# FNet plus top-1 MoE on one core: the products of one spectral unit split in two halves, the second moved behind the next unit

## The chip, the cores and the metric

The kernel runs on one core of one Trainium2 chip. The time is the device time of one execution in microseconds (us); the median of the runs is compared. PE is TensorE (matmuls), DVE is VectorE, ACT is ScalarE, POOL is GpSimd, SP is SyncE, which here issues nearly all loads. "Granted clock" is the share of its full clock that PE was given.

## What is computed

```
xn  = layernorm(x)                                   # x: 2048 x 512
a, b = xn @ dft_hid_re.T, xn @ dft_hid_im.T          # DFT over the hidden axis
y   = dft_seq_re @ a - dft_seq_im @ b                # real part of the DFT over the sequence
h_e = silu(xn @ w1[e]) @ w2[e]                       # 8 experts, 512 -> 1376 -> 512
out = x + y + gate * h_top1                          # each token by its top-1 expert of xn @ w_gate
```

All is float32. The kernel takes the sequence DFT first, on `xn`, and the hidden DFT last.

## The kernel before

**Precision by splitting.** A float32 operand is split into a high half `hi` (a cast, on ACT) and a low half `lo = v - hi` (a subtraction, on DVE), both of the type that PE takes in one pass. A product is then three matmuls: `hi x xh`, `lo x xh`, `hi x xl`, where `xh`, `xl` are the halves of the tokens (lines 537 to 539). One matmul of 128 x 128 by 128 x 512 is the unit of work here.

**Four units.** The sequence DFT's matrix is cut into chunks of 512 output rows; two neighbouring chunks `c` and `c + 1`, of the real matrix (`ri` 0) or of the imaginary one (`ri` 1), make a unit: `UNITS = [(0, 0), (0, 1), (1, 0), (1, 1)]`, pair and `ri`. In a unit a 2 x 2 block scheme saves one product in eight. It has an "even" half, run now, and an "odd" half, run behind the MoE. The even half (`EVEN`, line 522) makes four products for each of eight blocks `b` of 256 input rows: `p1` and `p2` of the block itself ("plain": one load of 512 KB, one cast, one low half), and `q6` and `p3` of sums of blocks ("sums": the plain block and a second load of 512 KB, `other`; three additions, lines 495 to 497; a cast and a low half, lines 470 and 474). Each product of a block is 6 matmuls, so a block has 24, 12 of them on the plain part and 12 on the sums. The two accumulators of each product stand in two PSUM banks; the eight banks hold one unit's four products. When a unit is done, `out_of` copies them on ACT to `raw` tiles and stores them.

**Order of the work.** `add` (line 100) lists all blocks once, in the order in which they are to be loaded and prepared; `need(key, ahead)` (line 104) writes out the preparation of every block up to `ahead` behind the one wanted. A scheduler then orders the instructions of each engine ahead of time, earlier-written ones first among those that it believes ready; each engine works through its own list in order, and an instruction that waits holds all behind it. SP's list is kept in the written order throughout (line 217); DVE's and ACT's are kept so only in the stretches marked `manual_schedule`. Slots: six `raw` tiles (shared by loads and by the stores of results), two `other`, two `sums`, four pairs of `hi` and `lo`.

**The (0,1) unit of before** has a lead: for the first six blocks (`LEAD = 6`) it does the plain products alone, from blocks of their own kind ("c"), two ahead. Meanwhile `between` (line 571) does, block by block, the logits of the router (`logits`, 128 small matmuls), their join and copy (`join_logits`), the choice of expert (`choose`), and the count of tokens per expert (`count`, two small matmuls whose result opens `route`). Then come the sums of these six blocks ("even" with `sums_alone`, line 501), and blocks 6 and 7 with all four products. During that and during the (1,0) unit `go_on` and `during` (lines 905 and 913) do the rest of the routing (`route`, small instructions on DVE in pieces), write the tokens as halves of words (`words`, ACT) and scatter them by expert (`scatter`, POOL, an indirect DMA each). In the (1,1) unit the first expert's window of tokens is loaded on SP, which needs all scatters done. The experts' MoE, the odd halves and the hidden DFT follow.

Of the kernel before, what the change touches and what calls it, by code (L numbers as in the profile page):

```python
# [23 lines left out]
NB = NT // 2  # L24
KD = D // P
TC = 512
# [6 lines left out]
DH = D // 2  # L33
UNITS = [(0, 0), (0, 1), (1, 0), (1, 1)]
PLAIN = 5
LEAD = 6
KS = D // 32


# [9 lines left out]
def fnet_moe(ctx, tc, x, cr, ci, dr, di, wg, w1, w1r, w2, w2r, out):  # L49
    nc = tc.nc  # L50
    V, A, T, G, SY = nc.vector, nc.scalar, nc.tensor, nc.gpsimd, nc.sync
# [9 lines left out]
    def bank(name):  # L61
        return psum.tile([P, 512], F32, tag="bank", name=name)
# [37 lines left out]
    def add(key, fn):  # L100
        order[key] = len(blocks)
        blocks.append((key, fn))

    def need(key, ahead):
        for i in range(len(ready), min(order[key] + 1 + ahead, len(blocks))):
            ready[blocks[i][0]] = blocks[i][1]()
        return ready[key]

    def c_block(c, ri, b):
        src = (cr, ci)[ri][c, b].rearrange("p j t -> p (j t)")  # L110
        add(("c", c, ri, b), lambda: stream(src, P, 1024))
# [14 lines left out]
    for b in range(PLAIN):  # L126
        for c in range(2):
            c_block(c, 0, b)
    for u in range(len(UNITS)):
        if u == 1:  # L130
            for b in range(LEAD):
                c_block(0, 1, b)
            for b in range(LEAD):
                add(("even", 1, b), lambda b=b: (None, sums_alone(b)))
        for b in range((PLAIN, LEAD, 0, 0)[u], NB):
            add(("even", u, b), lambda u=u, b=b: even_sums(u, b))
    for i in range(E):
        for b in range(6):
            for k in range(2):
# [326 lines left out]
    def two_parts(t, cols):  # L466
        hi = st.tile([P, 1024], F32R, tag="hi", name="hi")
        lo = st.tile([P, 1024], F32R, tag="lo", name="lo")
        n = cols.stop - cols.start
        A.copy(hi[:, :n], t[:, cols])  # L470
        return hi, lo, t, cols, n

    def low_parts(hi, lo, t, cols, n):
        V.tensor_sub(lo[:, :n], t[:, cols], hi[:, :n].bitcast(F32))  # L474
        return hi, lo
# [13 lines left out]
    def sums_of(u, b):  # L489
        if not tp:  # L490
            tp.append(ctx.enter_context(tc.tile_pool(name="two", bufs=2)))
        raw, other, t = raw_blocks(u, b, 0)

        def add_up():
            V.tensor_add(t[:, :TC], other[:, :TC], other[:, TC:])
            V.tensor_add(t[:, :TC], t[:, :TC], raw[:, :TC])
            V.tensor_add(t[:, TC:], t[:, :TC], raw[:, TC:])

        return raw, t, add_up

    def sums_alone(b):
        raw, t, add_up = sums_of(1, b)
        add_up()
        return low_parts(*two_parts(t, slice(0, 2 * TC)))

    def even_sums(u, b):
        raw, t, add_up = sums_of(u, b)
        plain = two_parts(raw, slice(0, 2 * TC))
        add_up()
        plain = low_parts(*plain)  # L510
        return plain, low_parts(*two_parts(t, slice(0, 2 * TC)))

    def odd_sums(u, b):
# [8 lines left out]
    EVEN = [(0, 0, 0, "p1"), (0, 1, 2, "p2"), (1, 0, 1, "q6"), (1, 1, 3, "p3")]  # L522
    ODD = [(0, 0, 2, "q4"), (1, 0, 3, "q5"), (1, 1, 1, "p7")]

    def product(todo, key, acc, b0=0, going=(), ahead=3):
        b = key[-1]
        got = need(key, ahead)
        if key[0] == "c":
            got = (got,)
        for m, n, q, name in todo:  # L530
            if name not in acc:
                acc[name] = [bank(f"s{k}") for k in range(2)]
            ch, cl = (v[:, n * TC:(n + 1) * TC] for v in got[m])
            for k in range(2):
                c = (q % 2) * DH + k * P
                a, al = xh[b][:, q // 2, c:c + P], xl[b][:, q // 2, c:c + P]
                T.matmul(acc[name][k], a, ch, start=(b == b0 and name not in going), stop=False)  # L537
                T.matmul(acc[name][k], a, cl, start=False, stop=False)  # L538
                T.matmul(acc[name][k], al, ch, start=False, stop=(b == NB - 1))  # L539

    def out_of(acc, u, names=None):
        for n in names or acc:
            store_pair(ps[n][u], acc[n])

    def unit(kind, u, mid=None, lead=0, between=None, acc=None):
        todo = {"even": EVEN, "odd": ODD}[kind]
        acc = acc or {}
        going = tuple(acc)
        b0 = 0 if u else PLAIN
        for b in range(lead):  # L550
            product(todo[:2], ("c", 0, 1, b), acc, ahead=2)
            between(b)
        for b in range(b0, NB):
            product(todo[2 if b < lead else 0:], (kind, u, b), acc, b0, going)
            if mid:
                mid(b)
        return acc

    plain = two_products(2, pre0)
# [4 lines left out]
    acc = unit("even", 0, go_on_first, acc={"p2": plain[:2], "p3": plain[2:]})  # L564
# [4 lines left out]
    written = ExitStack()  # L569

    def between(b):
        if b < 2:
            if b == 1:
                logits()
                written.enter_context(tc.manual_schedule(engines={A.engine}))
                copy_logits()
            turn_some((), (3 + b,))
            return
        if b == LEAD - 1:
            count()  # L580
        if b > 2:
            spread(b - 3)
            return
        written.close()
        join_logits()
        early.close()
        late.append(early.enter_context(tc.tile_pool(name="late", bufs=1, side="right")))
        zero = late[0].tile([P, D], F32, name="zero")
        G.memset(zero, 0.0)
        for t, base, n in ((xs, S, 3 * P), (hr, WCUM[E], 1)):  # L590
            for r in range(0, n, P):
                m = min(P, n - r)
                tc.keep_in_program_order(A.dma_start(t[base + r:base + r + m, :], zero[:m, :].bitcast(U16)))
        with tc.high_priority(), tc.manual_schedule(engines={V.engine}):
            choose()

    def sm(name, shape, dt=F32):
        return late[0].tile([P] + shape, dt, name=name)
# [4 lines left out]
    def choose():  # L603
        top = sm("top", [NT])
        V.reduce_max(top, lg, axis=AX.X)

        is_top = sm("is_top", [NT, E])
        V.tensor_tensor(is_top, lg, top[:, :, None].to_broadcast([P, NT, E]), op=OP.is_equal)
        V.tensor_mul(is_top, is_top, per_tile(down1))
        ftop = sm("ftop", [NT])  # L610
        V.reduce_max(ftop, is_top, axis=AX.X)
        V.tensor_tensor(oh, is_top, ftop[:, :, None].to_broadcast([P, NT, E]), op=OP.is_equal)

        gd = sm("gd", [NT])
        ge_gr.extend((sm("ge", [NT]), sm("gr", [NT])))
        ge = ge_gr[0]
        V.tensor_sub(gd, top, top)
        A.activation(ge, gd, AF.Exp)
# [10 lines left out]
    routing = []  # L629

    def count():
        cnt = parts4[2]
        ohf = oh.rearrange("p t e -> p (t e)")
        T.matmul(cnt[:, 0:P], ones, ohf, start=True, stop=True)
        T.matmul(cnt[:, P:2 * P], before, ohf, start=True, stop=True)
        routing.append(route(cnt))
        with tc.high_priority():
            next(routing[0])

    def scan(name, t0, n, steps):  # L640

        t = [t0, sm(name, list(t0.shape[1:]))]
        q = 0
        for sh in steps:
            V.tensor_copy(t[1 - q][:, :sh], t[q][:, :sh])
            V.tensor_add(t[1 - q][:, sh:], t[q][:, sh:], t[q][:, :n - sh])
            q = 1 - q
        return t[q]
# [7 lines left out]
    def route(cnt):  # L656
        tot = sm("tot", [NT, E])
        V.tensor_copy(tot.rearrange("p t e -> p (t e)"), cnt[:, 0:P])
        rank = sm("rank", [NT, E])
        V.tensor_sub(rank.rearrange("p t e -> p (t e)"), cnt[:, P:2 * P], tot.rearrange("p t e -> p (t e)"))  # L660
        inc = scan("inc1", tot, NT, (1, 2, 4, 8))
        V.tensor_add(rank, rank, inc)
        num, num1 = sm("num", [E]), sm("num1", [E])
# [234 lines left out]
    def spread(*tiles):  # L898
        for t in tiles:
            words(t)  # L900
            if routing:
                for o in range(len(scat), t + 1):
                    scatter(o)

    def go_on(b):
        spread(*((3,), (4,), (5,), (6,), (7,), (), (), ())[b])
        if b >= LEAD - 1:
            next(routing[0], None)

    acc = unit("even", 1, go_on, LEAD, between)  # L910
    out_of(acc, 1)

    def during(b):
        next(routing[0], None)
        spread(*((8, 9), (10, 11), (12, 13), (14,), (15,), (), (), ())[b])
        if b == 6:
            place(0)

    acc = unit("even", 2, during)
    out_of(acc, 2)  # L920
    early.close()
    norms_on.close()
    mo = ExitStack()
# [15 lines left out]
    acc = unit("even", 3, during_last)  # L939
# [5 lines left out]
    todo = []  # L945
# [123 lines left out]
    for u, mid in enumerate((None, load_ds, first_fetches, last_fetches)):  # L1069
        acc = unit("odd", u, mid)  # L1070
# [143 lines left out]
```

## Time and profile before

| | |
|---|---|
| median of 3 runs | 696.73 us (695.53 to 698.81) |
| the profiled execution | 697.55 us, of which the span from the first to the last instruction is 695.8 |
| PE busy | 684.8 us, 98% of the span |
| DVE busy | 551.1 us, 79% |
| ACT busy | 403.6 us, 58% |
| moved by DMA | 174.31 MB, 251 GB/s in the mean |
| mean granted clock of PE | 0.995 |

A row of the timeline gives the start (us from the span's start), the time taken, the engine, the source line, the operation, the tile written and the tiles read, shapes, a count where equal neighbours are merged, and in brackets how long the engine had been idle before it and what ended that. In a row of waits stand who waited for whom, the total in us, how often, and the longest. In a row of stretches stand the busy time of each engine with its number of instructions, then the granted clock, the busy share of the 16 DMA engines and GB/s. A busy PE says only that matmuls were in flight; their pitch, from one start to the next, tells at what speed.

### The profile page before, as it was taken

The numbers are of one execution on the slowest core, as the hardware profiler recorded it, in microseconds if no ns is written. First come the engines' busy times: TensorE is split into PE (matmuls) and PEld (weight loads), VectorE is DVE, ScalarE is ACT, GpSimd is POOL, SyncE is SP. The second block draws the span as 40 slices with busy tenths as digits, with TensorE's granted clock in tenths as the row PEclk, the third lists the DMA queues.
The fourth block names the chain that finished last, engine by engine and source line by source line (L and its number), as shares of the span: only waits on it lengthen the run. The fifth ranks groups of instructions, "written<-read, shape, count | busy, mean of one in ns | idle before, by whom it ended". The sixth has DMA issues, their size and how long they took to land.

```text
span 695.8 us, 10899 instructions
## 1 busy us (share of the span) xinstructions
PE 684.8 (98%) x3859; PEld 598.7 (86%) x3859; DVE 551.1 (79%) x912; ACT 403.6 (58%) x628; POOL 55.9 (8%) x66
## 2 busy tenths in 40 slices
PE   9999979999999999999999999999999999999997
PEld 7888758888888999999999999999888878888886
DVE  6979869999685767777778697878779799658784
ACT  5684636757557466656666676664556464425342
POOL 1000001418100000000000000000000000222120
PEclk9999989999999999999999999999999999999999
DMA  9464686898893976685985868747496988689775
GB/s 320 179 231 151 218 304 222 340 380 289 257 311 114 303 243 181 220 180 199 264 274 166 282 171 286 251 138 263 144 329 218 350 320 309 233 325 362 250 266 177
DMA packets 88184, 174.31 MB, mean 251 GB/s; under 512 B 40318, under 2 KB 41598, under 8 KB 88125
## 3 DMA queue, kind: packets, MB, share of 16 engines
q1 hardware_dynamic: 77691, 143.02, 63.4%
q10 hardware_dynamic: 7874, 22.16, 8.4%
q0 software_dynamic: 2560, 8.39, 3.4%
q8 instruction: 32, 0.52, 0.3%
q14 instruction: 27, 0.22, 0.1%
HBM read 135.59 MB, written 29.42 MB: 237 GB/s over the span
## 4 chain that ended last, share of the span: by engine, by line
PE 67%; DVE 14%; DMA 12%; ACT 3%; issue 2%; SPq 0%; DVEq 0%; ACTq 0%
PE s L538 7%; PE s L539 7%; PE s L537 7%; PE up L831 6%; PE up L830 6%; PE acc L343 6%; PE up L829 6%; PE y L860 4%; PE y L861 4%; PE y L859 4%; DVE lo L474 2%; PE y L852 2%; PE y L853 2%; PE y L854 2%; DMA raw<-pd 2%
## 5 line engine op out<-in xcount | busy, mean ns | idle before, releaser
L81 DVE TENSOR_TENSOR lo<-raw,hi 128x1024 fp32r<-128x1024 f32 (+2 forms) x109 | 123.0, 1133 | 36.2 <-ACT hi L80 34.4
L538 PE MATMUL s<-lo,xh 128*128 128x512 f32 x366 | 144.1, 394 | 5.0 <-DVE lo L81 4.5
L80 ACT CAST hi<-raw 128x1024 fp32r<-128x1024 f32 (+2 forms) x109 | 106.9, 987 | 62.8 <-PE up L830 34.8
L539 PE MATMUL s<-hi,xl 128*128 128x512 f32 x366 | 143.3, 392 | 0.0
L537 PE MATMUL s<-hi,xh 128*128 128x512 f32 x366 | 140.1, 393 | 0.0
L830 PE MATMUL up<-wtl,hi 128*128 128x256 f32 (+10 forms) x352 | 102.4, 291 | 0.0
L831 PE MATMUL up<-wth,lo 128*128 128x256 f32 (+10 forms) x352 | 102.4, 291 | 0.0
L829 PE MATMUL up<-wth,hi 128*128 128x256 f32 (+10 forms) x352 | 102.3, 291 | 0.0
L470 ACT CAST hi<-sums 128x1024 fp32r<-128x1024 f32 x54 | 57.0, 1055 | 76.2 <-PE s L539 32.9
L538 PEld LDWEIGHTS s<-lo,xh 128*128 128x128 f32 x366 | 69.4, 190 | 21.1 <-DVE lo L81 4.9
L537 PEld LDWEIGHTS s<-hi,xh 128*128 128x128 f32 x366 | 69.2, 189 | 16.5 <-issue 1.7
L474 DVE TENSOR_TENSOR lo<-sums,hi 128x1024 fp32r<-128x1024 f32 x54 | 66.1, 1223 | 21.0 <-ACT hi L470 20.8
L539 PEld LDWEIGHTS s<-hi,xl 128*128 128x128 f32 x366 | 69.4, 190 | 14.4
L829 PEld LDWEIGHTS up<-wth,hi 128*128 128x128 f32 (+1 forms) x352 | 66.0, 187 | 1.3
L830 PEld LDWEIGHTS up<-wtl,hi 128*128 128x128 f32 (+1 forms) x352 | 66.0, 187 | 1.3
L831 PEld LDWEIGHTS up<-wth,lo 128*128 128x128 f32 (+1 forms) x352 | 66.0, 188 | 0.0
L860 PE MATMUL y<-hl,hi 128*128 128x318 f32 (+9 forms) x220 | 65.2, 297 | 0.2 <-DVE hl L837 0.2
L861 PE MATMUL y<-hh,lo 128*128 128x318 f32 (+9 forms) x220 | 65.0, 296 | 0.0
L859 PE MATMUL y<-hh,hi 128*128 128x318 f32 (+9 forms) x220 | 64.2, 296 | 0.0
L1084 POOL DMA_INDIRECT hw<-hr,posr x16 | 20.9, 1306 | 478.2 <-PE s L539 424.0
L833 ACT ACTIVATE sil<-up 128x256 f32<-128x256 f32 (+9 forms) x88 | 35.5, 404 | 32.1 <-PE up L831 17.9
L470 ACT CAST hi<-raw 128x512 fp32r<-128x512 f32 (+1 forms) x48 | 38.9, 811 | 22.6 <-PE s L539 9.4
(232 smaller groups left out, 1288.7 us busy)
## 6 DMA issues: line engine op xcount, KB each, us to landing
raw<-in_w SPq DMA_DIRECT2D x80, 512.0 KB
raw<-in_ci SPq DMA_DIRECT2D x38, 512.0 KB
raw<-in_cr SPq DMA_DIRECT2D x30, 512.0 KB
p<-raw ACTq DMA_DIRECT2D x16, 512.0 KB
other<-in_ci SPq DMA_DIRECT2D x16, 512.0 KB
q<-raw ACTq DMA_DIRECT2D x12, 512.0 KB
other<-in_cr SPq DMA_DIRECT2D x11, 512.0 KB
other<-p SPq DMA_DIRECT2D x10, 512.0 KB
```

The costliest lines, as they stand in the source:

```text
L80: A.copy(hi, raw)
L81: V.tensor_sub(lo, raw, hi.bitcast(F32))
L470: A.copy(hi[:, :n], t[:, cols])
L537: T.matmul(acc[name][k], a, ch, start=(b == b0 and name not in going), stop=False)
L538: T.matmul(acc[name][k], a, cl, start=False, stop=False)
L539: T.matmul(acc[name][k], al, ch, start=False, stop=(b == NB - 1))
L829: T.matmul(t[:m, :w], hi[:, c:c + m], self.xh[:, k, :w], start=(k == 0), stop=False)
L830: T.matmul(t[:m, :w], hi[:, c:c + m], self.xl[:, k, :w], start=False, stop=False)
L831: T.matmul(t[:m, :w], lo[:, c:c + m], self.xh[:, k, :w], start=False, stop=(k == KD - 1))
L859: T.matmul(y, hi[:m, c:c + P], hh[:m, :w], start=first, stop=False)
L860: T.matmul(y, hi[:m, c:c + P], hl[:m, :w], start=False, stop=False)
L861: T.matmul(y, lo[:m, c:c + P], hh[:m, :w], start=False, stop=last)
```

## The change

- The (0,1) unit is cut in two. `plain_half` does the plain products of all eight blocks, from blocks of the "c" kind, two ahead, and stores `p1` and `p2`. Then the whole (1,0) unit runs. Then `unit("alone", 1)` does the sums' products of (0,1), all eight blocks, and stores `q6` and `p3`. The list of blocks is put in that order.
- `between` is called for all eight blocks of the plain half. The count stands behind block 5 as before, now behind the words of that block, and the piece of `route` that ends in the tokens' places (`posi`) is cut off from it by a `yield` and done behind block 6. From `choose` to the end of the plain half DVE's list is kept in the written order (before: only within `choose`, with raised priority).
- The further pieces of `route` are done in the (1,0) unit; words and scatters: tokens' tiles 0 to 4 in the plain half, 5 to 12 in (1,0), 13 to 15 in the sums alone, where also the first expert's place is read.
- In `even_sums` the low half of the plain block is written ahead of the three additions, not behind them.

```diff
-LEAD = 6
+COUNT = 5
...
-    for u in range(len(UNITS)):
-        if u == 1:
-            for b in range(LEAD):
+    for u in (0, 2, 3):
+        for b in range(0 if u else PLAIN, NB):
+            add(("even", u, b), lambda u=u, b=b: even_sums(u, b))
+        for b in range(NB):
+            if u == 0:
                 c_block(0, 1, b)
-            for b in range(LEAD):
-                add(("even", 1, b), lambda b=b: (None, sums_alone(b)))
-        for b in range((PLAIN, LEAD, 0, 0)[u], NB):
-            add(("even", u, b), lambda u=u, b=b: even_sums(u, b))
+            if u == 2:
+                add(("alone", 1, b), lambda b=b: (None, sums_alone(b)))
...
     def even_sums(u, b):
         raw, t, add_up = sums_of(u, b)
-        plain = two_parts(raw, slice(0, 2 * TC))
+        plain = low_parts(*two_parts(raw, slice(0, 2 * TC)))
         add_up()
-        plain = low_parts(*plain)
...
+    def plain_half(mid):
+        acc = {}
+        for b in range(NB):
+            product(EVEN[:2], ("c", 0, 1, b), acc, ahead=2)
+            mid(b)
         return acc
...
-        if b == LEAD - 1:
-            count()
         if b > 2:
+            if b == COUNT + 1:
+                next(routing[0])
             spread(b - 3)
+            if b == COUNT:
+                count()
             return
...
-        with tc.high_priority(), tc.manual_schedule(engines={V.engine}):
-            choose()
+        written.enter_context(tc.manual_schedule(engines={V.engine}))
+        choose()
...
+        yield
         inc = scan("inc1", tot, NT, (1, 2, 4, 8))
...
-    acc = unit("even", 1, go_on, LEAD, between)
+    acc = plain_half(between)
+    written.close()
     out_of(acc, 1)
 
     def during(b):
         next(routing[0], None)
-        spread(*((8, 9), (10, 11), (12, 13), (14,), (15,), (), (), ())[b])
+        spread(b + 5)
+
+    acc = unit("even", 2, during)
+    out_of(acc, 2)
+
+    def meanwhile(b):
+        spread(*((13,), (), (14,), (), (15,), (), (), ())[b])
         if b == 6:
             place(0)
 
-    acc = unit("even", 2, during)
-    out_of(acc, 2)
+    acc = unit("alone", 1, meanwhile)
+    out_of(acc, 1)
```

More of the change, by code (lines that the diff above doesn't have):

```diff
@@ L543, in out_of, with unit @@
             store_pair(ps[n][u], acc[n])
-    def unit(kind, u, mid=None, lead=0, between=None, acc=None):
-        todo = {"even": EVEN, "odd": ODD}[kind]
+    def unit(kind, u, mid=None, acc=None):
+        todo = {"even": EVEN, "odd": ODD, "alone": EVEN[2:]}[kind]
         acc = acc or {}
@@ L549, in unit @@
         b0 = 0 if u else PLAIN
-        for b in range(lead):
-            product(todo[:2], ("c", 0, 1, b), acc, ahead=2)
-            between(b)
         for b in range(b0, NB):
-            product(todo[2 if b < lead else 0:], (kind, u, b), acc, b0, going)
+            product(todo, (kind, u, b), acc, b0, going)
             if mid:
                 mid(b)
+        return acc
+    def plain_half(mid):
[3 more added lines that the diff above has]
+            mid(b)
         return acc
@@ L903, in spread @@
                     scatter(o)
[L905 to L908, printed above, removed]
-    acc = unit("even", 1, go_on, LEAD, between)
+    acc = plain_half(between)
+    written.close()
     out_of(acc, 1)
```

## The prediction

> **What bounds the kernel now.** I read the page's first part first, then the table of what TensorE (PE) waited for, then a table by stretches of 5 us, then the timelines of PE, VectorE (DVE) and ScalarE (ACT) around the one place that stood out.
>
> ```profile
> span 695.8 us, 10899 instructions
> PE 684.8 (98%) x3859; PEld 598.7 (86%) x3859; DVE 551.1 (79%) x912; ACT 403.6 (58%) x628; POOL 55.9 (8%) x66
> ```
>
> PE is busy in all but 11.0 us of the span. Nothing in this change takes away or adds a matmul, so all that it can win is PE's idle time and time in which matmuls ran slowly. The waits of PE, whole run:
>
> ```profile
> PE s L538 <- DVE lo L81: 4.5, 1, 4.5
> PE spare L208 <- DVE eps L211: 1.1, 1, 1.1
> PE s L538 <- DVE lo L474: 0.5, 1, 0.5
> ```
>
> The columns are who waited for whom, total us, times, longest. One wait of 4.5 us is most of what can be had (1.1 is the start). L81 is the low half of a streamed block, so the waiting product is a plain one of the (0,1) unit. The stretches around it (PE busy, weight loads, DVE, ACT, POOL, granted clock, DMA share, GB/s):
>
> ```profile
> 90.00:95.00 5.00, 4.77 (x24) 2.69 (x22) 2.08 (x3) 3.01 (x4) 0.00 (x0) 1.00 0.96 339
> 95.00:100.00 5.00, 0.72 (x2) 0.63 (x3) 4.32 (x7) 1.05 (x2) 0.00 (x0) 0.83 0.92 324
> 100.00:105.00 5.00, 5.00 (x14) 3.83 (x13) 5.00 (x9) 1.14 (x3) 0.53 (x1) 0.50 0.56 218
> 105.00:110.00 5.00, 5.00 (x24) 3.99 (x23) 4.21 (x17) 4.82 (x8) 0.00 (x0) 0.99 0.93 329
> ```
>
> After the gap PE counts as fully busy from 100 to 105, but does 14 matmuls where an undisturbed stretch does 22 (5 us at 0.2267 us each), at a granted clock of 0.50. PE's own rows (start, us):
>
> ```profile
> 94.38 0.39 PE L537 MATMUL s<-hi,xh 128*128 128x512 f32 x1
> 99.28 0.79 PE L538 MATMUL s<-lo,xh 128*128 128x512 f32 x1 [4.52 <-DVE lo L81]
> 99.88 0.63 PE L539 MATMUL s<-hi,xl 128*128 128x512 f32 x1
> ...
> 104.57 0.63 PE L538 MATMUL s<-lo,xh 128*128 128x512 f32 x1
> 105.28 0.39 PE L537 MATMUL s<-hi,xh 128*128 128x512 f32 x1
> ...
> 107.09 0.39 PE L539 MATMUL s<-hi,xl 128*128 128x512 f32 x1
> ```
>
> From 105.28 to 107.09 lie 8 steps of 0.226 us (0.2267 over longer runs: the pitch). 94.38 to 107.09 are the 24 matmuls of plain blocks 4 and 5; at the pitch they take 24 x 0.2267 = 5.44 us, and they took 107.09 + 0.23 - 94.38 = 12.94. **Loss: 7.5 us**: about 4.7 of waiting, and 2.8 of half-speed matmuls.
>
> Why the low half came late (DVE and ACT):
>
> ```profile
> 86.64 0.43 DVE L450 TENSOR_TENSOR tb<-tb,xn 128x256 f32<-128x256 f32 x1
> 91.72 0.69 DVE L495 TENSOR_TENSOR sums<-other 128x512 f32<-128x512 f32 x1 [4.65 <-DMA other<-in_ci]
> ...
> 95.62 0.69 DVE L495 TENSOR_TENSOR sums<-other 128x512 f32<-128x512 f32 x1 [1.75 <-DMA other<-in_ci]
> ...
> 98.01 1.22 DVE L81 TENSOR_TENSOR lo<-raw,hi 128x1024 fp32r<-128x1024 f32 x1
> ```
> ```profile
> 89.94 2.02 ACT L80 CAST hi<-raw 128x1024 fp32r<-128x1024 f32 x2
> ```
>
> Both high halves were made by 91.96. The low half stood in DVE's queue behind the add-ups of two sums blocks, which waited 4.65 and 1.75 us for transfers that the plain blocks do not need.
>
> **The change part by part.** *Plain products first.* Ahead of plain block 4 now stand only plain blocks, each one transfer and one low half; no add-up is issued until plain block 6 asks two ahead. The wait of 4.5 us and the slow clock behind it go: 7.5 us off, if the next-latest thing holds. That is the count: the block after it needs `oh`, made by the chain that starts when the logits are joined.
>
> ```profile
> 90.52 1.06 PE L414 MATMUL part<-turned,sel 128*32 128x512 f32 x8
> ```
> ```profile
> 99.15 0.71 DVE L417 STREAM_TRANSPOSE turned<-part 128x512 f32<-128x512 f32 x1
> ...
> 105.88 0.29 DVE L612 TENSOR_TENSOR oh<-is_top,ftop 128x128 bf16<-128x128 f32 x1
> ```
>
> The join ends at 91.6. The transpose (0.71) and six instructions of at most 0.29 give `oh` near 94.1; the count stands on PE behind plain block 5, which now ends at 94.38 + 5.44 = 99.8. Spare: 5.7 us. The low half of plain block 5, now in order behind `choose`, comes at 94.1 + 0.2 + 1.2 = 95.5, due at 97.1: 1.6 spare. So the plain half runs through, and its blocks 6 and 7 end at 99.8 + 0.1 + 5.44 = 105.4. The logits and the join are unmoved on PE.
>
> *The (1,0) unit* follows: 192 matmuls, 43.5 us, to 148.9. *Then the moved part*: 8 blocks of sums alone, each 12 matmuls, 2.72 us, 21.8 us in all. Each needs two transfers of 512 KB, as this one (1.05 MB together), three additions, a cast and a low half. Before, six such blocks stood in the (0,1) unit, after PE had waited for them.
>
> ```profile
> raw<-in_ci SPq DMA_DIRECT2D x38, 512.0 KB
> ```
>
> DVE's steps at full pace:
>
> ```profile
> 161.46 0.68 DVE L495 TENSOR_TENSOR sums<-other 128x512 f32<-128x512 f32 x1
> 162.06 0.68 DVE L497 TENSOR_TENSOR sums<-sums,raw 128x512 f32<-128x512 f32 x1
> 162.67 1.21 DVE L474 TENSOR_TENSOR lo<-raw,hi 128x1024 fp32r<-128x1024 f32 x1
> 163.80 0.68 DVE L496 TENSOR_TENSOR sums<-sums,raw 128x512 f32<-128x512 f32 x1
> ```
>
> An addition holds DVE 0.60 us, a low half 1.13. A sums block alone is 3 x 0.60 + 1.13 = 2.93 us against 2.72 of PE; a full block is 4.06 against 5.44. Routing, over the stretch that holds it (rows of L474 and of one of the three equal additions):
>
> ```profile
> 107.64:158.59 50.95, 21.84 (x19) 1.00 0.87 320
> ...
> 107.64:158.59 50.95, 7.58 (x11) 1.00 0.87 320
> ```
>
> 50.95 - 19 x 1.13 - 33 x 0.60 = 9.7 us, from the count's first reader to the last table. DVE's account behind the count (100.2): eight full blocks 32.5, eight sums alone 23.4, routing 9.7, two waits for a cast of 1.01 (2.02 for two, above) because DVE now follows the written order through the first two (1,0) blocks, and the last block's own cast 1.0: 68.6, so 168.8. PE wants the last low half at 148.9 + 7 x 2.72 = 167.9. DVE is 0.9 us short if no transfer ever holds it, nothing if PE does the four high products (0.9) first, as it does where a low half is expected late:
>
> ```profile
> 121.25 1.08 PE L537 MATMUL s<-hi,xh 128*128 128x512 f32 x4
> ```
>
> *Transfers there.* SP, the load queue, works in written order, and its raw tiles share six slots with the stores. At the unit boundary of before (1,0 to 1,1):
>
> ```profile
> 174.53 1.06 ACT L363 COPY raw<-s 128x512 f32<-128x512 f32 x2
> ```
> ```profile
> 178.33 0.33 SPq L481 DMA_DIRECT2D raw<-in_ci  x1
> 178.76 0.37 SPq L486 DMA_DIRECT2D other<-in_ci  x1
> ```
> ```profile
> 184.11 0.69 DVE L495 TENSOR_TENSOR sums<-other 128x512 f32<-128x512 f32 x1
> ```
> ```profile
> SPq L481 <- DMA p<-raw: 14.9, 3, 11.1
> ```
>
> The first eviction starts when the first product of the last block is done, 18 matmuls (4.1 us) ahead of the unit's end T = 178.6. The fourth block's raw load was held up to 11.1 us for a store and left at T - 0.3; its first addition ran at T + 5.5. Before, that block was due 16 us after T; a fourth sums block is due at T + 8.2. From its first addition it needs 3 x 0.60 + 1.0 + 1.2 + some 0.2 of hand-overs = 4.2 us: T + 9.7, 1.5 late. The four blocks behind it go at DVE's 2.93 against 2.72: 0.8 more. This and DVE's account are the same queue, so they do not add. I take 2.5 us, near this row's 2.3; the ends are 0 (three blocks ready ahead cover it) and 5.4 (below). The gaps would be under 2 us each; the 0.5 us wait of the list above left the clock alone:
>
> ```profile
> 560.00:565.00 5.00, 4.55 (x21) 3.49 (x20) 5.00 (x7) 2.62 (x4) 0.00 (x0) 1.00 0.94 355
> ```
>
> Gaps between 0.5 and 4.5 us the trace does not show. By the Trainium skill (TensorE: Matmul & The Clock Gate, Part 1) the clock halves only after about 3.4 us idle and recovers after about 3.4 us of work; the trace agrees with the first in its 4.5 us wait and shows a longer recovery, 5.9 us. By that rule gaps under 2 us cost only themselves, as I count them.
>
> *The rest.* The low half written ahead of the add-up in full blocks costs nothing of its own: ACT's cast (1.01) is hidden by PE's three-block lead, and if it is not, 1.0 us for each such block. The eight words and scatters per unit shift later by a few blocks: the last scatter would be issued in the fifth sums-alone block, 10 us ahead of the (1,1) unit, whose second block holds the window load that waits for it; an SP wait there would hold the later loads of (1,1). POOL, whose scatters go in order, then has the same work over a longer stretch. PSUM: the sums alone take four banks, and those that they take over were evicted three products before. I cost these at nothing.
>
> **Sum.** 7.5 - 2.5 = 5.0 us gained. The profiled execution took 697.55 us, 1.75 around its span; the median of the runs is 696.73. 697.55 - 5.0 = 692.55, and on the median **691.7 us**.
>
> **The rivals.** *Transfers bound the sums alone.* From T - 0.3 must arrive five blocks of 1.05 MB, three stores of 0.52 and three scatters of 0.26: 7.6 MB. Over the fullest 25 us of before the 16 engines moved:
>
> ```profile
> 140.00:165.00 25.00, 25.00 (x112) 20.70 (x111) 25.00 (x73) 17.13 (x25) 9.43 (x5) 1.00 1.00 374
> ```
>
> 7.6 MB at 374 GB/s is 20.3 us; the last block lands at T + 20.0, is ready at T + 24.4, due at T + 19.0: 5.4 us lost, 2.1 gained, 694.6. For it: DMA share 1.00 there. Against: three blocks are loaded before T. The Trainium skill (DMA: Bandwidth & Descriptors, Where 436 GB/s comes from) has loads from HBM bound by about 358 GB/s per core; by that figure 0.9 us more would be lost. The 374 here stands above it.
>
> *The plain half still waits.* If the low half of block 4 is ordered behind something slow (the join, the parts of x), a wait of 2 us stays: 2.7 or so of the idle goes, 2.8 of clock may stay or not. With the 2.5 lost later, 0.2 to 3.0 gained: about 695.
>
> *Slower.* The raw load of the fourth sums block is late, as at the boundary from (0,1) to (1,0), 43.5 us ahead of the other, at 135.1:
>
> ```profile
> 137.39 0.33 SPq L481 DMA_DIRECT2D raw<-in_cr  x1
> ```
> ```profile
> 146.77 0.68 DVE L495 TENSOR_TENSOR sums<-other 128x512 f32<-128x512 f32 x1
> ```
>
> There the fourth block's load left at T + 2.3 and its first addition ran at T + 11.7. With the 4.2 us behind it, a sums block would be ready at T + 15.9, 7.7 late; the clock would halve (2.8), and DVE's 0.8 follows: 11.3, of which the gain covers 7.5: 3.8 slower, 700.5. It decides from one gap of about 4.5 us in the sums alone. Against it: DVE was busy with routing in that stretch, and there is little routing left then.
>
> **How the numbers follow.** Forecast 0.60 (0 to 4 us lost: 689.2 to 693.2), transfers 0.18, plain half 0.12, slower 0.10. Under 0.5% (3.5 us) a measurement of this kernel cannot tell from no change. So faster 0.60; same 0.18 + 0.12 = 0.30; slower 0.10. The range goes from 688.8 (nothing lost, and the 0.4 of small waits gone) to 698.5, which leaves out the slower case and little else; the likeliest case alone is 689.2 to 693.2.
>
> **What would show it.** Right: no PE wait on L81, granted clock 1.00 from 85 to 110, the plain half ended near 105; DVE full from the count on; PE waits on L474 in the sums alone, 2 to 3 us in several gaps, clock 1.00. Wrong: a PE wait of over 4 us anywhere in the two units, an SP wait on a store just ahead of the fourth sums block that reaches PE, or DVE waiting for `other` there.

## The result and the profile after

The changed kernel takes 704.25 us in the median (703.96 to 705.15, 4 runs) beside 696.33 for the kernel before (695.53 to 698.81, 4 runs): ratio 1.011, interval 1.0082 to 1.0138. It is slower by 1.1%; 691.7 was forecast. The first part of the page, then the largest of what TensorE (PE) waited for:

```profile
span 702.8 us, 10909 instructions
PE 684.5 (97%) x3859; PEld 598.1 (85%) x3859; DVE 553.1 (79%) x912; ACT 402.1 (57%) x628; POOL 50.3 (7%) x66
```
```profile
PE s L537 <- DVE lo L474: 8.5, 4, 5.5
PE s L536 <- ACT hi L470: 2.5, 2, 2.0
```

The work of PE is the same as before; its idle time went from 11.0 to 18.3 us. The wait on L81 is gone. In its place stand six waits for the halves of blocks (L470 casts a high half, L474 subtracts a low one). Where they lie is read from the same stretches of both kernels (columns as above: PE, weight loads, DVE, ACT, POOL, granted clock, DMA share, GB/s), before first:

```profile
85.00:108.00 23.00, 18.48 (x148) 12.71 (x125) 15.59 (x28) 10.48 (x18) 0.53 (x1) 0.85 0.86 307
108.00:130.00 22.00, 21.93 (x96) 17.61 (x95) 21.73 (x55) 13.58 (x20) 9.45 (x7) 1.00 0.79 281
150.00:185.00 35.00, 35.00 (x156) 29.00 (x155) 31.20 (x47) 26.48 (x38) 20.77 (x9) 1.00 0.82 291
```
```profile
85.00:108.00 23.00, 23.00 (x184) 17.13 (x176) 14.12 (x26) 15.50 (x25) 0.53 (x1) 1.00 0.72 256
108.00:130.00 22.00, 18.17 (x78) 14.07 (x77) 21.83 (x64) 11.10 (x16) 12.93 (x6) 1.00 0.82 299
130.00:150.00 20.00, 20.00 (x90) 16.56 (x89) 20.00 (x61) 11.00 (x16) 5.48 (x4) 1.00 0.73 267
150.00:185.00 35.00, 27.75 (x112) 21.57 (x111) 24.69 (x33) 18.62 (x30) 7.07 (x6) 0.90 0.91 338
```

- *Plain half* (85 to 108): PE never stops and the clock stays at 1.00. Before, 4.5 us of idle and 2.8 of half clock (18.48 x 0.15) lay here: about 7.3 us gained, as forecast (7.5).
- *Start of (1,0)* (108 to 130): 3.83 us idle against 0.07: 3.8 lost. Nothing was forecast here.
- *Sums alone* (from T = 154.3): 7.25 us idle, and a lower clock around the longest gap, by these rows of the changed kernel:

```profile
165.00:170.00 5.00, 1.96 (x8) 0.95 (x6) 0.17 (x1) 1.05 (x1) 0.00 (x0) 0.92 1.03 418
170.00:175.00 5.00, 1.92 (x5) 1.54 (x6) 4.20 (x6) 1.29 (x2) 0.00 (x0) 0.50 1.01 387
175.00:180.00 5.00, 5.00 (x21) 4.12 (x20) 4.97 (x7) 1.85 (x3) 1.20 (x1) 0.89 0.99 351
```

1.96 x 0.08 + 1.92 x 0.50 + 5.00 x 0.11 = 1.7 us of PE's busy time lost to it. 8.9 lost in all; 2.5 was forecast.

7.3 - 3.8 - 8.9 = -5.4 by idle time and clock, while the span grew by 7.0. Idle time hides short waits, because a matmul counts as busy for the 0.39 us that it is in flight, while the next can start 0.2267 us behind it. The starts of matmuls show these waits too: the (1,0) unit takes 48.3 us where 43.5 were forecast, and the sums alone take 31.6 (first and last row below, with the fifth and the sixth block between) where 96 matmuls at the pitch take 21.8.

```profile
154.32 0.39 PE L536 MATMUL s<-hi,xh 128*128 128x512 f32 x1
...
166.35 1.20 PE L536 MATMUL s<-hi,xh 128*128 128x512 f32 x4 [0.60 <-ACT hi L470]
...
176.39 1.09 PE L536 MATMUL s<-hi,xh 128*128 128x512 f32 x4
...
185.94 0.39 PE L536 MATMUL s<-hi,xh 128*128 128x512 f32 x1
```

That is 7.3 - 4.7 - 9.8 = -7.2, and the (1,1) unit starts 7.1 us later than before (185.9 against 178.8).

At the start of (1,0), VectorE's own rows show what stands ahead of the low half that PE wants (the second block's):

```profile
108.68 0.17 DVE L650 COPY inc<-tot 128x8 f32<-128x8 f32 x1
...
112.90 0.17 DVE L677 TENSOR_TENSOR posi<-rrk,rro 128x16 int32<-128x16 f32 x1
113.00 1.23 DVE L474 TENSOR_TENSOR lo<-raw,hi 128x1024 fp32r<-128x1024 f32 x1
```

The chain of the tokens' places holds DVE from 108.68 to 113.0, 4.3 us, and the low half is written behind it. In the sums alone, PE, DVE and then the load queue:

```profile
173.08 0.80 PE L537 MATMUL s<-lo,xh 128*128 128x512 f32 x1 [5.52 <-DVE lo L474]
```
```profile
152.13 0.69 DVE L495 TENSOR_TENSOR sums<-other 128x512 f32<-128x512 f32 x1
...
158.62 0.69 DVE L495 TENSOR_TENSOR sums<-other 128x512 f32<-128x512 f32 x1 [0.89 <-DMA other<-in_ci]
159.35 0.69 DVE L496 TENSOR_TENSOR sums<-sums,raw 128x512 f32<-128x512 f32 x1
...
164.48 0.69 DVE L497 TENSOR_TENSOR sums<-sums,raw 128x512 f32<-128x512 f32 x1
170.47 0.69 DVE L495 TENSOR_TENSOR sums<-other 128x512 f32<-128x512 f32 x1 [5.30 <-DMA other<-in_ci]
171.19 0.69 DVE L496 TENSOR_TENSOR sums<-sums,raw 128x512 f32<-128x512 f32 x1
171.80 1.22 DVE L474 TENSOR_TENSOR lo<-sums,hi 128x1024 fp32r<-128x1024 f32 x1
```
```profile
157.68 0.33 SPq L481 DMA_DIRECT2D raw<-in_ci  x1
166.18 0.33 SPq L486 DMA_DIRECT2D other<-in_ci  x1
```
```profile
SPq L486 <- DVE sums L495: 32.4, 13, 9.5
...
SPq L486 <- DMA p<-raw: 8.1, 1, 8.1
```

This is the old wait in a new place. The additions at 152.13, 158.62 and 170.47 open the third, the fourth and the sixth block. The low half at 171.80 belongs to the fifth block, whose high half ended at 166.3, but it stands in DVE's queue behind additions of the sixth, which wait 5.3 us for `other`. That load left 8.5 us behind the one ahead of it, 8.1 of them spent waiting for a store (last row: the load queue from 95 to 200 us; the row above it shows that most of its waiting is for VectorE to free a tile). Why it waits for a store is told by the list of its waits in the built program, where it is load 66:

```
66 L486 DMA other<-in_ci 128x1024 [waits DMAHW5_49,DMAHW2_49,DVE_49]
```

In that program the loads of SP and the stores of ACT use eight such transfer counters (DMAHW0 to 7) in turn, and counter 2 had last been used by the store of `p2`, issued at 158.0. The tile's own slot had been free since 159.3, when the fourth block's first addition ended.

### The profile page after: what moved, and what is told of

The parts are those of the page before. It is cut to its first block, busy times and chain, and to the rows that moved or that the text cites. A ratio compares the mean times of both kernels' runs of the same rounds, so it can differ in the third digit from the quotient of the medians.

```text
span 702.8 us, 10909 instructions
## 1 busy us (share of the span) xinstructions
PE 684.5 (97%) x3859; PEld 598.1 (85%) x3859; DVE 553.1 (79%) x912; ACT 402.1 (57%) x628; POOL 50.3 (7%) x66
## 4 chain that ended last, share of the span: by engine, by line
PE 80%; DVE 9%; DMA 5%; ACT 4%; issue 1%; ACTq 0%; SPq 0%; DVEq 0%
PE s L537 8%; PE s L538 8%; PE s L536 8%; PE up L837 6%; PE acc L343 6%; PE up L836 6%; PE up L835 6%; PE o L1115 4%; PE o L1113 4%; PE o L1114 4%; PE y L866 4%; PE y L867 4%; PE y L865 4%; DVE lo L474 3%; PE y L858 2%; PE y L859 2%
## 5 line engine op out<-in xcount | busy, mean ns | idle before, releaser
L81 DVE TENSOR_TENSOR lo<-raw,hi 128x1024 fp32r<-128x1024 f32 (+2 forms) x111 | 125.5, 1135 | 40.9 <-ACT hi L80 38.9
L80 ACT CAST hi<-raw 128x1024 fp32r<-128x1024 f32 (+2 forms) x111 | 108.5, 985 | 64.5 <-PE up L836 36.2
L536 PE MATMUL s<-hi,xh 128*128 128x512 f32 x366 | 137.5, 391 | 2.5 <-ACT hi L470 2.5
L470 ACT CAST hi<-sums 128x1024 fp32r<-128x1024 f32 x54 | 56.9, 1053 | 87.8 <-DVE sums L497 37.3
L474 DVE TENSOR_TENSOR lo<-sums,hi 128x1024 fp32r<-128x1024 f32 x54 | 66.0, 1222 | 19.1 <-ACT hi L470 18.8
L1092 POOL DMA_INDIRECT hw<-hr,posr x16 | 18.5, 1158 | 472.8 <-PE s L538 418.6
L470 ACT CAST hi<-raw 128x512 fp32r<-128x512 f32 (+1 forms) x46 | 36.7, 797 | 16.5 <-PE s L538 5.3
```

What stands on the lines that cost most here:

```text
L80: A.copy(hi, raw)
L81: V.tensor_sub(lo, raw, hi.bitcast(F32))
```

## The experiments

A first theory (S) was the ties of loads to stores: by that counter, and by the six `raw` slots that both use. Its rivals were the bytes (B, later T), VectorE's work (D), and the place of the blocks. Each run stands beside runs of the kernel before on its own chip, and the ratio is to these. The kernel before took 695.3 to 696.7 us on these chips, so a difference of two medians from different chips is good to about 1.4 us.

### Is it the ties? x1, x5, x6, y4

**x1**: POOL issues the four stores of (1,0), with counters of other queues. `store_pair(..., by=G)`: `by.dma_start(dst, o)` for `A.dma_start(dst, o)`.

> The changed kernel, with the four stores of the (1,0) unit's results issued by POOL instead of ACT: the same bytes, at the same place, but in the built program SP's loads of the sums-alone blocks then no longer wait for the completion counters that these stores use. Theory A (a load held for a store): the gap of 5.5 us and the 2.8 us of half clock behind it come from the second load of the sixth sums-alone block, which left at 166.2, when a store had landed, though its tile was free at 159.3. Then the gap falls to under 1.5 us, the clock stays, and the time is 695 to 697. Rival B (too many bytes at once): the 16 engines are full from 155 to 180 in any case, the load lands as late, and the time stays within 2 us of 704.3.

704.87, ratio 1.013 (1.0066 to 1.0193): nothing won, the time that rival B gave. But now a `raw` load was held, for the store that had its slot:

```profile
SPq L481 <- DMA p<-raw: 7.3, 1, 7.3
```

So freeing the counter alone does not help: the shared slot does the same.

**x5**: both ties cut: as x1, and two of the four results are stored from tiles of their own.

```diff
-        o = raw_tile()
+        o = late[0].tile([P, 1024], F32, name="kept", bufs=2) if own else raw_tile()
```

> The changed kernel, with the stores of (1,0) freed of both ties to the loads: p1 and p2 are copied to two tiles of their own instead of two of the six raw tiles, and all four are issued by POOL. In the built program no load of sums-alone blocks 3 to 6 (counted from 0) waits for a store any more; the bytes are the same. Theory S (loads are held by stores, by a tile or by a counter): the gap of 4 to 6 us in the sums alone shrinks to under 1.5 us, the clock stays, time 695 to 698. Rival B (bytes: loads and stores together fill the engines) and rival D (the sums alone want more than DVE and its two slots of each kind give): a gap of over 3 us and the fall of the clock stay, time over 702.

700.73, ratio 1.0058 (1.0029 to 1.0086), between the two expectations. The ties cost about 3.5 us, and their cure is not the whole. Start of (1,0) and sums alone:

```profile
108.00:130.00 22.00, 18.32 (x72) 13.95 (x71) 21.83 (x64) 11.10 (x15) 12.93 (x6) 0.92 0.79 290
150.00:185.00 35.00, 32.03 (x134) 25.56 (x133) 28.24 (x37) 22.25 (x35) 10.09 (x10) 0.95 0.98 367
```

**x6 and y4**: only 32 of the 1024 columns of these four stores are written, to scratch memory; the rest is left out, and what reads them later takes the results of (0,0). In x6 all four go to one scratch tile, in y4 to four.

> The changed kernel, storing only 32 of the 1024 columns of each of (1,0)'s four results, to a place that is never read; later reads take the results of (0,0) in their stead (2 MB of stores are left out, reads are as many as before). Theory S or rival B: tiles and counters come free at once and the bytes are gone; the gap shrinks to under 1.5 us and the time is 695 to 697. Rival D: the gap stays above 3 us. Read together with the run that frees the ties at the same bytes: S if both lose the gap, B if only this one does, D if neither does.

> The changed kernel with 32 of 1024 columns of each of the four (1,0) stores, each to a tile of memory of its own; 31/32 of these stores is left out, and what reads the four later takes the results of (0,0). Rival B (the bytes of the four stores crowd the loads of the sums alone): the wait of a load on a store falls under 2 us, the late gap of 5.5 under 1.5, and the time is 695 to 698. Theory D with the ties (order, not bytes): the late gap stays at 3 us or more and the time at 701 to 704.

x6 702.36, ratio 1.0092 (1.0067 to 1.0117), but its four stores wait for each other, so it says little. y4 700.52, ratio 1.0077 (1.006 to 1.0093): neither expectation was met. A load still waited 6.5 us for a store of 16 KB (`SPq L492 <- DMA aside<-raw: 6.5, 1, 6.5`): that wait is order more than bytes. The late gaps fell to 2.6 and 1.7, so the bytes of the stores count too; whether directly or because a small store ends the tie earlier, the run does not tell.

### What cured the plain half? x2, x4, x8

**x2**: VectorE's written order only within `choose`, with raised priority, as in the kernel before; the rest of the change stays.

> The changed kernel, with DVE kept in the written order only within the choice of experts (as before the change), and not to the end of the plain half. Theory: the 3.8 us that PE lost in the first two blocks of (1,0) come from the written order, in which the chain to the tokens' places stands ahead of the second block's low half; freed, the scheduler puts the low halves first, and the time falls by 3 to 4 us, to about 700.5. Rival: DVE has that work to do there in any order, and the time stays within 1 us of 704.3. The later gap of 5.5 us should stay in both.

707.3, ratio 1.0153 (1.0104 to 1.0201); neither expectation came true, because the wait on L81 is back.

```profile
101.03 0.80 PE L537 MATMUL s<-lo,xh 128*128 128x512 f32 x1 [5.88 <-DVE lo L81]
```

So the written order cures that wait, not the split of the unit: without it an addition of the first (1,0) block, waiting 7.5 us for its transfer, still came ahead of the low half. The gaps at the start of (1,0) are gone in x2, as its theory had it, but PE comes to that unit 8 us later, so the order and the later start are not told apart.

**x4**: x1 and x2 together.

> Both edits of the first two: the stores of (1,0) issued by POOL, and DVE's written order only within the choice of experts. If the two losses are separate, as the theory has it, the savings add: 8 and 3.5 us off 704.3, so 692 to 693.5, faster than before the change. If both are one shortage of DVE that moves from place to place, the sum of both is no better than the better of the two.

707.25, ratio 1.0163 (1.0116 to 1.0209). PE waits 6.0 us on L81 and up to 5.2 at once on L474. Alone neither edit had saved anything, and together they do not either.

**x8**: the kernel before, with only the written order added (from `choose` to the count), no block moved.

> The kernel before, with one thing of the change: DVE's list kept in the written order from the choice of experts to the count; no block is moved. Theory: the wait on L81 (7.5 us with the clock) came from the order of DVE's list and goes; but the stalled PE had let DVE get ahead, so of the 7.5 us some 3 to 6 come back as waits for the sums: 692 to 695. Rival 1 (DVE is the limit from there to (1,0) in any order): all 7.5 come back, 696 to 698. Rival 2 (the order is all): 689 to 690.

696.03, ratio 1.0007 (0.9978 to 1.0037). The 4.5 us wait is gone, yet nothing is won that the interval shows:

```profile
104.63 0.96 PE L537 MATMUL s<-hi,xh 128*128 128x512 f32 x3 [2.39 <-ACT hi L470]
```

The half clock follows this wait too (0.66 from 105 to 110). That the old wait had given the sums time to catch up fits this, and is argued only.

### Is it the place? x3, x7, y1

**x3**: the sums alone directly behind the plain half, ahead of (1,0).

> The changed kernel, with the eight sums-alone blocks directly behind the plain half, ahead of the (1,0) unit (so not two units on); the stores of (1,0) then fall ahead of (1,1), whose blocks take PE 5.4 us each. Theory A or B of the late gap: it goes (5.5, 1.1, 0.6 and 2.8 us), and instead DVE is short at the start of the sums, where routing, three additions and a low half for 2.7 us of PE come together: 4 to 6 us lost. Time 698 to 700. Rival (the move two units on is what spares DVE, as the change has it): the shortage there is over 10 us with a fall of the clock, and the time is over 704.

707.88, ratio 1.0174 (1.0128 to 1.022): the theory was missed, and the rival's case came. PE's gaps add up to 10 us, all directly behind the plain half, the longest 5.8; none come later. So the place two units on is not itself the fault.

**x7**: the chain of places one block later, behind the second (1,0) block:

```diff
             if b == COUNT + 1:
+                words(b - 3)
+                return
+            if b == NB - 1:
                 next(routing[0])
```

> The changed kernel, with the chain to the tokens' places (the piece of the routing behind the count) written one block later, behind the preparation of (1,0)'s second block, and the scatters with it. Theory: PE's 3.8 us in (1,0)'s second block come from this chain's place in DVE's written order; they shrink to under 1 us and the time falls by 3 to 4 us, or, if the sums alone behind take it all back, by nothing, with a longer gap there. Rival: DVE is short there by its work and the loss stays where it is.

703.81, ratio 1.0111 (1.005 to 1.0173). The start loses 0.6 us in place of 3.8, which shows that this chain was its cause. The late stretch is no better, with 7.7 us idle, and DVE is busier there than in the changed kernel (27.90 against 24.69):

```profile
108.00:130.00 22.00, 21.43 (x94) 17.04 (x93) 20.73 (x58) 10.31 (x14) 2.69 (x3) 1.00 0.59 214
150.00:185.00 35.00, 27.33 (x108) 20.72 (x107) 27.90 (x37) 20.50 (x30) 7.93 (x6) 0.95 0.97 364
```

The profiled execution (701.57) was the shortest of four; the median shows next to nothing of the 3.2 us won at the start, but the interval is too wide to say how much came through.

**y1**: x5 and x7 together.

> The changed kernel with both cures in one: two of the (1,0) stores from tiles of their own and all four issued by POOL (alone 700.7), and the places' chain one block later (alone 703.8). Theory D (VectorE is short of lead from the end of the plain half to the end of the sums alone, and TensorE's waits move but add up to much the same): 697 to 701, waits for high and low halves still 5 to 8 us in all over both units. Rival S (the late gap is only the tie of a load to a store): the start loses 0.5, the late blocks under 2, and the time is 694 to 696.5.

700.62, ratio 1.0076 (1.0058 to 1.0094). With the ties cut and the start cured, 5.1 us of idle stay in the sums alone, at a full clock. Theory S does not suffice: something else binds there.

### What binds the sums alone? y2, y3, z1, z2, z3

VectorE was full from 108 to 150, so the next theory (D) was its work. **y2** gives the first of three additions of each block of sums alone to POOL in x8, **y3** in y1: `add_up(G)`.

> The kernel before with VectorE's order from choose to the count as written (alone 696.0, waits of 2.4 us and less) and the first of the three additions of each block of the sums alone moved to POOL. Theory D: VectorE is relieved of 8 x 0.69 us in the sums alone, nothing there waits on it, and since the plain half lies behind the sums alone here, VectorE comes into it with more lead: 691 to 694. Rival S (VectorE is not short): 695.5 to 697, or slower if POOL's addition takes so long, several us each, that the halves come later: 698 to 705.

> The first kernel of this batch with the first addition of each block of the sums alone on POOL. Theory D: the late waits for a half fall under 2 us in all and the time goes 3 to 5 us below that of the first: 692 to 697. Rival S: no change against the first within 1 us. If POOL's addition is much slower than VectorE's 0.69 us: the sums come later, and both units lose more, 700 or above.

y2 698.65, ratio 1.0048 (1.0031 to 1.0064); y3 707.4, ratio 1.0181 (1.0155 to 1.0207). Both were slower than what they started from (y2 by little: its interval just touches that of x8). An addition takes POOL 1.3 to 2.3 us where DVE needs 0.69, and the block comes later. That does not clear DVE, so the next three runs each take one thing alone out of y1.

**z1**: no raw load in the sums alone; VectorE adds zeros in its place.

```diff
-            V.tensor_add(t[:, :TC], t[:, :TC], raw[:, :TC])
+            V.tensor_add(t[:, :TC], t[:, :TC], raw[:, :TC] if load else zeros[0][:, :TC])
```

> On y1_own_and_later (700.6, waits for halves of 5.7 us, nearly all in the sums alone): the sums alone load no raw tile and add a tile of zeros in its place, so that VectorE does the same additions and the unit loads half the bytes (its sums lack the raw part). Theory T (the transfers bind the sums alone: 1.05 MB per block of 2.9 us, 416 to 420 GB/s measured): late waits under 1 us in all, time 694.5 to 697. Theory D (VectorE's work binds): waits stay over 4 us, 699.5 to 701.5. Theory R (the loop of two slots of other binds, a load of 2.7 us or more after VectorE has freed its slot): faster loads shorten the loop, waits of 1 to 3 us, 696 to 698.5.

**z2**: the first addition left out, all loads kept (`V.tensor_add(t[:, :TC], other[:, :TC], raw[:, :TC])` opens the sum).

> On y1_own_and_later: the sums alone leave out the first of three additions of each block (0.69 us of VectorE; the sums lack one of four parts), all loads as before. Theory D: late waits under 2 us, 695.5 to 698. Theory T: bytes unchanged, waits 4 us or more, 699.5 to 701.5. Theory R: the slot of other is freed at the same addition, waits 4 us or more, 699 to 701.

**z3**: a third slot for `other` (`late[0] if b % 3 == 2`).

> On y1_own_and_later: in the sums alone, every third tile other comes from a slot of its own, so that three loads can be ahead instead of two (for room, six tiles of words in place of eight). Nothing is left out. Theory R: late waits under 2 us, 695.5 to 698. Theory T: 699.5 to 701.5, the transfers at 415 GB/s or more as before, only earlier by a block, at best 1 to 2 us less wait. Theory D: 699.5 to 701.5.

The last column is the time of the eight sums alone, by the starts of PE's matmuls; at the pitch it would be 21.8.

| | median us | ratio (interval) | sums alone, us |
|---|---|---|---|
| y1 | 700.62 | 1.0076 (1.0058 to 1.0094) | 30.2 |
| z1 | 696.05 | 1.0001 (0.997 to 1.0031) | 25.3 |
| z2 | 700.82 | 1.008 (1.0056 to 1.0105) | 29.9 |
| z3 | 699.38 | 1.006 (1.004 to 1.0081) | 28.1 |

The same 25 us of the sums alone, in y1, z1, z2 and z3:

```profile
155.00:180.00 25.00, 20.15 (x78) 13.74 (x79) 20.12 (x26) 12.46 (x18) 6.77 (x6) 1.00 1.01 395
```
```profile
155.00:180.00 25.00, 24.46 (x99) 17.68 (x98) 24.44 (x32) 17.13 (x25) 7.47 (x6) 1.00 0.97 360
```
```profile
155.00:180.00 25.00, 20.55 (x80) 15.27 (x79) 16.05 (x19) 12.53 (x19) 6.89 (x8) 0.93 1.02 402
```
```profile
155.00:180.00 25.00, 22.20 (x87) 15.20 (x86) 21.98 (x29) 14.43 (x21) 7.97 (x6) 1.00 1.01 398
```

In y1 the 16 DMA engines are busy throughout while PE stands for 4.9 of 25 us. With less work for VectorE (third line) VectorE is idle for 9 us and PE still stands for 4.5: D fell. With fewer bytes (second line) PE's idle time falls to 0.5, and 4.6 us are won by the medians, 4.8 in the stage: the transfers bind (T). A slot more (fourth line) takes 2.1 us off the stage in the profiled execution; the 1.2 us between the medians are within the noise. So the two slots (R in the expectations) bind a little too. In z1 VectorE is busy 24.44 of 25 us, and the stage still takes 3.6 us more than at the pitch: VectorE is the next bound, close behind. z1 also frees slots of `raw` tiles. These did not hold y1: from 130 to 185 us its raw loads waited 0.2 us in all for a slot.

### Can it be used? z4, w1, w2

If bytes bind where sums come in a row, these sums should be spread. **z4**: x8 with two more slots of `other`. **w1** and **w2**: x8, and behind the six plain halves of (0,1) the two full blocks stand among the six sums alone (w1) or ahead of them (w2). Nothing is left out in them and the bytes are those of the kernel before.

```diff
+SUMS = (6, 0, 1, 7, 2, 3, 4, 5)
...
-            for b in range(LEAD):
-                add(("even", 1, b), lambda b=b: (None, sums_alone(b)))
+            for b in SUMS:
+                add(("even", 1, b), lambda b=b: (None, sums_alone(b)) if b < LEAD else even_sums(1, b))
```

> The kernel before with VectorE's order written from choose to the count (alone 696.0, waits of 2.4, 0.3 and 0.3 us in the sums alone), and every second tile other of the sums alone from two slots of its own, four in all. Theory R: these waits fall under 1 us and the clock stays up, 692.5 to 694.5, faster than the kernel before. Theories T and D: 695 to 697, as alone.

> The kernel before with VectorE's order written from choose to the count (alone 696.0, span 693.7), and in the (0,1) im unit the blocks behind the six plain halves in the order 6, 0, 1, 7, 2, 3, 4, 5: the two full blocks among the sums alone instead of behind them. Theory T (bytes): behind the plain halves a full block gives 2.7 us more before the first sums are due and 5.4 us for its 1.05 MB, so the wait of 2.4 us and the half clock behind it (about 1.7) go: 692 to 694, faster than the kernel before. If the count's chain or VectorE's queue binds there instead: 695.5 to 698.

> The same with the order 6, 7, 0, 1, 2, 3, 4, 5: both full blocks first. Theory T: the first wait goes too, but six sums alone in a row, at 2.5 us of transfers for 2.7 of TensorE with only two tiles other ahead, stand against the stores and loads at the unit's end: small waits come back late in the unit, 692.5 to 695.5, not faster than the first. If VectorE's queue binds: it has more lead here, 692 to 694, faster than the first.

| | median us | ratio (interval) |
|---|---|---|
| z4 | 696.4 | 1.0027 (1.0003 to 1.0051) |
| w1 | 693.53 | 0.9942 (0.9919 to 0.9965) |
| w2 (6, 7, 0, 1, ...) | 694.58 | 0.9964 (0.9936 to 0.9992) |

In z4 PE waited 3.0 us at 105 with the transfers at 417 and 418 GB/s: more slots did not help while the engines were full. w1 beats both kernels, and x8 too. From its page, and the waits of PE:

```profile
span 691.4 us, 10904 instructions
```
```profile
PE spare L210 <- DVE eps L213: 1.1, 1, 1.1
PE up L833 <- ACT hi L81: 0.5, 1, 0.5
PE s L541 <- DVE lo L476: 0.5, 2, 0.3
```

No gap above 0.3 us is left in this stage, and the clock stays at 1.00. A full block takes 5.4 us of PE for the 1.05 MB that sums alone must get in 2.7. w2 has small waits of 0.2 to 0.65 us; it is not clearly slower than w1. These two runs show that spreading helps, not that bytes alone are why: a full block also gives VectorE 5.4 us for its 4.1 us of additions and low halves, where a sums block gives 2.7 for 2.9. And full engines alone do not stop PE: from 130 to 135 w1 moves 419 GB/s and PE has no gap.

## Why the prediction was wrong

- **The plain half** was right in cause and size: 7.5 us forecast, 7.3 measured, no wait on L81, clock 1.00. It named the order of the list of blocks as the cure; x2 and x8 showed that VectorE's written order is what does it: without it the wait came back, and with it alone the wait went.
- **Behind the count** the account of VectorE had the routing in its sum of 9.7 us, but not in its place. "Two waits for a cast of 1.01" was all that the written order was to cost; the 4.3 us of the places' chain stand in one piece ahead of the second block's low half, and PE lost 3.8. x7 took all but 0.6 of this away by moving the chain.
- **The sums alone** are the step that failed: 2.5 us forecast, 8.9 measured by idle time and clock, 9.8 by the starts. The forecast had the fourth block 1.5 late and "the four blocks behind it go at DVE's 2.93 against 2.72: 0.8 more". Up to the fourth block it held: three blocks were loaded before T = 154.3 (the third's first addition ran at 152.13), the fourth's first addition ran at T + 4.3 (forecast T + 5.5), and its low half was ready at T + 8.8 (forecast T + 9.7). The term for the four blocks behind it is what failed: it took VectorE's work as their pace and let no transfer hold them. From the fourth low half to the eighth went 20.8 us (163.1 to 183.9), 5.2 a block and not 2.93. The fifth block alone took PE 10.0 us, behind the load that a store held for 8.1. With these ties cut, 3.5 us of the whole came back (x5); with fewer bytes on top, 4.6 more (z1). A block's 1.05 MB take 2.5 us at 418 GB/s against 2.72 of PE, and stores and scatters want the same engines, so a lead once lost is hardly won back: curing the start (y1 beside x5) let T come 4.1 us earlier in the profiled execution, and the sums alone ended only 0.9 earlier. Even the pace of 2.93 was too short: in z1, where VectorE binds, the later blocks take 3.07 each, because an addition that reads the one ahead starts 0.73 behind it (158.62 and 159.35 above), not 0.60.
- **The rivals.** "Transfers bound the sums alone" named the mechanism that z1 shows, and priced it at 5.4 us (its own terms, T + 20.0 and 4.2, give 5.2). "Three blocks are loaded before T" was the argument against it; they were, and the transfers bound all the same. "Slower" had the right kind of event, one gap above 4.5 us from a load held by a store, and 700.5; it was the sixth block's `other` and not the fourth's raw tile. Both came, and the start's loss with them: 704.25.
- **The clock.** Gaps were to stay under 2 us and cost only themselves; the one of 5.52 brought the clock to 0.50. The Trainium skill (TensorE: Matmul & The Clock Gate, Part 1) has the clock halve after at least one idle window of about 3.4 us. The gap is longer than that, but the clock fell 1.7 us into it (gap from 167.6, half clock from 169.2): less idle than the page says was enough, as the last section shows.

What stays open: how the 3.5 us of the ties divide between counter and slots, how w1's gain divides between bytes and VectorE, and how a kernel would run that has w1's spread and the plain half of all eight blocks.

## What to carry to other kernels

A wait of one engine may give another engine, or the transfers, the time to get ahead for the next stage; before such a wait is counted as gain, work out the bytes and the instructions of the stage behind it against its own time, not against a mean over the span. Splitting a block into a half that needs no second load and a half that needs two leaves one stretch with transfers to spare and the other short of them: spread the short blocks among full ones. Small work put into a written order counts at its place in the queue, not in a sum.

## What the runs showed of the hardware

- Transfers of one core reached 416 to 420 GB/s over 5 us and 418 over 10 (y1, below). The Trainium skill (DMA: Bandwidth & Descriptors, Where 436 GB/s comes from) gives about 358 GB/s as a core's share of its memory and 435 as the limit of the ports; here the transfers, most of them loads, ran near the second, with one core used by the program.

```profile
160.00:170.00 10.00, 5.88 (x23) 3.58 (x22) 6.93 (x10) 3.13 (x4) 2.04 (x2) 1.00 1.03 418
```

- In all twenty traces the granted clock changed only at steps of 3.41 us: within these units the half clock lasted 3.4 us (x5, x7, x8, z2, z4), 6.8 (before, after, x2, x4) or 10.2 (x1). What decided was how long PE stood within the step of 3.41 us ahead of the fall, and not the length of one gap. At full clock, every step with 1.9 us or more of idle time was followed by half clock (2.2 in the changed kernel, 2.45 in x8, 1.98 and 1.91 in x5), and none with 1.5 or less; in between both are seen. So in the changed kernel the gaps of 1.71 and 1.95 could leave the clock at 1.00: the second fell across two steps (1.63 and 0.32 of it).
- A load waited 8.1 us for a store that touched nothing of its own, by a shared counter of transfers.
